# Experts' tails computed row by row, list building divided between one expert and the rest, and a softplus on other engines

## The chip, the cores and the metric

The kernel runs on one core of one Trainium2 chip. The metric is the device time of one execution in microseconds, and the median over several runs is compared. A profile of a single execution goes with it. Five engines matter: TensorE (PE, with PEld for its weight loads), VectorE (DVE), ScalarE (ACT), GpSimd (POOL), and SyncE (SP), which issues most DMAs.

## What is computed

Three stages follow each other (the reference, cut):

```python
for t in range(S):                                   # B=4, H=8, S=768, D=48
    state = alpha[:, :, t, :, None] * state + einsum('bhd,bhe->bhde', k[:, :, t], v[:, :, t])
    y[:, :, t] = einsum('bhd,bhde->bhe', q[:, :, t], state)
x = y as [3072, 384]
noisy = x @ w_gate + log1p(exp(x @ w_noise)) * noise          # 8 experts
top2 of noisy per token; softmax of the two values as weights
for e in range(8):                                            # w1[e] 384x1024, w2[e] 1024x384
    out[rows of e] += weight * (relu(x[rows of e] @ w1[e]) @ w2[e])
return ((out @ w_a) * (out @ w_b)) @ w_out                    # inner width 1536
```

## The kernel before, in words

Products of the expert and the last stage are in fp32 quality: each operand is split into a high and a low part, and `prod3` (L632 to L637) issues three matmuls for one product, on lines L635, L636 and L637. All engines run their instructions in program order, and that order is written out by hand.

**Attention, 24 tiles of 128 tokens.** In step i of the loop, `prep(i+3)` makes two scans on VectorE (D, L460, and A, L464) and two products on GpSimd into the ring of inputs (L462, L465); `sc_unit` (matmuls L490) makes the scores of the next tile, and VectorE masks them into `pm` (L495, two per tile); `intra` (L514) uses `pm`; `u_unit` (L537) and `s_unit` (L549 to L553, the last on GpSimd) carry the state; `gx_unit` and `gm_unit` (L559, L570) make the logits of the gate. Four times in each step `tick()` advances the generators in the list `side` by one piece. `w_tick` loads and splits the first expert's weights into W, one 128x384 piece a step, the split on ScalarE (L112) and GpSimd (L113). It loads at steps 3 to 18 and splits at steps 6 to 21 (`W_FIRST`).

**Routing in two groups, of 14 and 10 tiles.** `route(g)` is such a generator. It computes the softplus as ln(w) with a correction (L229 to L251: two operations on ScalarE, nine on VectorE, all on 128 x 14·8 = 128x112 elements in the first group), the top two (L256 to L264), the ranks by a scan and three matmuls (L270 to L290), and then the lists of tokens for all eight experts: in pieces of at most five tiles, VectorE compares 128 lanes (`at`) and 56 keys (`eqk`, eight experts by seven blocks) with the slots of both choices (L321), multiplies by the token's number (`bt`, L326), and PE sums them (L333). The first group has three such pieces, the second two. Between issue and use lie a few ticks (`LAG`, `RLAG`). `gather` (L368) then fetches 128 rows of x by an indirect DMA that POOL issues.

**Experts.** Expert 0 takes 512 rows from the first 14 tiles, which it can work on while the second group is routed, then 384 rows more. Experts 1 to 7 have 768 rows and a tail of 64 more that is computed only if a flag in `tails` says that the expert has more than 768 tokens. `up_unit` multiplies with w1 (nine matmuls for 128 outputs and 384 or 512 rows), ScalarE (L652) and VectorE (L653) write h into HB; `down_unit` multiplies with w2 (24 matmuls of 384 columns for 128 rows). `up_tail` (L657) holds, under an If on PE (L663), 72 matmuls of 64 columns, with w1 as the stationary operand; its Else is one matmul of 512 columns (L670). `down_tail` (L675) is the last down under a second If. `x_unit` (L376 to L379) transposes the gathered rows of the next expert into X in three PE transposes each.

**Around the experts.** `values_load` reads the eight flags into registers, on all engines for `over` (L853) and on PE for the seven `tails` (L854), all in one place between expert 0's last down and expert 1's first up. Until the experts' end, `bg()` decodes pieces of the last stage's weights, 36 in all, a new one at every third call, on ScalarE (L771, L772, L779), VectorE, GpSimd and two DMAs. Expert 7 goes: up for 512 rows, four downs, the gathers of the last stage's first block, up for 256 rows, `up_tail`, the weighted sums `x2_sum`, the other downs, and with them `split_more` for 36 pieces of the last stage's weights. Then come eight blocks of the last stage (`up2_unit`, `down2_unit`).

Of the kernel before, what the change touches and what calls it, by code (L numbers as in the profile page):

```python
# [36 lines left out]
LAG = 2, 4  # L37
RLAG = 4, 6
HOT = 5
W_FIRST = 3, 6  # L40
# [21 lines left out]
def moe_kernel(ctx: ExitStack, tc, qka0, qka1, afirst, v, wgn, noise, w1, w2, w3, out):  # L62
# [37 lines left out]
    idx = tl(const, [128, E * NJ], I32, "idx")  # L100
    flag = tl(const, [1, 1], I32, "flag")
# [40 lines left out]
    def w_tick(i):  # L142

        if 0 <= i - W_FIRST[0] < 2 * NF1:
            w_load()
        if 0 <= i - W_FIRST[1] < 2 * NF1:
            w_split()
# [23 lines left out]
    idxa = tl(rt, [128, CAPA // 128], I32, "idxa")  # L171
# [44 lines left out]
    def route(g):  # L216
# [10 lines left out]

        gl = tmp("gl", 16)
# [3 lines left out]
        az, ex, w, c, r, ln = (tmp(x) for x in ("az", "ex", "w", "c", "r", "ln"))  # L232
        nc.vector.scalar_tensor_tensor(az, z, -1.0, z, op0=ALU.mult, op1=ALU.max)
        yield
        yield
        nc.scalar.activation(ex, az, AF.Exp, scale=-1.0)
        yield
        yield
        nc.vector.tensor_scalar(w, ex, 1.0, None, op0=ALU.add)
        yield  # L240
        nc.scalar.activation(ln, w, AF.Ln)
# [3 lines left out]
        yield  # L245
        yield
        sp, nl = tmp("sp"), tmp("nl")
        nc.vector.tensor_tensor(sp, ln, c, op=ALU.subtract)
        nc.vector.scalar_tensor_tensor(sp, z, 0.0, sp, op0=ALU.max, op1=ALU.add)
        nc.vector.tensor_tensor(nl, sp, noise_t[:, i0:i0 + n], op=ALU.mult)  # L250
        nc.vector.tensor_tensor(nl, nl, lg, op=ALU.add)  # L251
        yield
        ms, ohs = [], []
        for k in range(2):
# [3 lines left out]
            nc.vector.tensor_tensor(eq, nl, m[:, :, None].to_broadcast(sh), op=ALU.is_equal)  # L258
            nc.vector.tensor_tensor(eq, eq, prio[:, None, :].to_broadcast(sh), op=ALU.mult)
            nc.vector.tensor_reduce(mk, eq, axis=AX.X, op=ALU.max)  # L260
            nc.vector.tensor_tensor(oh, eq, mk[:, :, None].to_broadcast(sh), op=ALU.is_equal)
            if k == 0:
                nl2 = tmp("nl2")
                nc.vector.scalar_tensor_tensor(nl2, oh, -1e30, nl, op0=ALU.mult, op1=ALU.add)  # L264
                nl = nl2
                yield
            ms.append(m)
            ohs.append(oh)
        yield
        nc.vector.tensor_tensor(dm[:, i0:i0 + n], ms[1], ms[0], op=ALU.subtract)  # L270
        oa, xc = tl(rt, [128, E, n + 1], F32, f"oa{n}"), tl(rt, [128, E, n + 1], F32, f"xc{n}", bufs=2)
# [4 lines left out]
        oav = oa[:, :, 1:].rearrange("p e j -> p j e")  # L276
        nc.vector.tensor_tensor(oav, ohs[0], ohs[1], op=ALU.add)
# [3 lines left out]
        for _ in range(RLAG[last]):  # L281
            yield
# [18 lines left out]
        for k in range(2):  # L301
            t = tmp("t")
            nc.vector.tensor_tensor(t, ohs[k], rs, op=ALU.mult)
            nc.vector.tensor_reduce(sf[:, :, k], t, axis=AX.X, op=ALU.add)
        sl = slot[:, i0:i0 + n]
        nc.vector.tensor_copy(sl, sf)
        yield
        pi, ki, pf, kf = tmp("pi", 2, I32), tmp("ki", 2, I32), tmp("pf", 2), tmp("kf", 2)
        nc.vector.tensor_scalar(pi, sl, 127, None, op0=ALU.bitwise_and)
        nc.vector.tensor_scalar(ki, sl, 7, None, op0=ALU.logical_shift_right)  # L310
        nc.vector.tensor_copy(pf, pi)
        nc.vector.tensor_copy(kf, ki)
        yield

        for j0 in range(0, n, HOT):
            m = min(HOT, n - j0)
# [558 lines left out]
    while decs:  # L875
        bg()
# [178 lines left out]
```

## Time and profile before

| what | value |
|---|---|
| three runs | 1122.39, 1128.95, 1122.89 us |
| median | 1122.89 us |
| profiled execution, its own time | 1125.76 us |
| its span | 1124.0 us |
| mean granted TensorE clock | 0.965 of full speed |

The profiled execution takes 1.8 us beyond its span and 2.9 us beyond the median of the runs. The clock is a share of 2.4 GHz: 1.00 is that level, 0.50 would be the level of 1.2 GHz, and a number between says that a stretch had both. PE's columns count a matmul as busy while it is in the pipeline, so that busy matmuls may still be slow ones.

### The profile page before, as it was taken

The page shows a single profiled execution, that of the slowest core. Times are in us where ns is not written, and L with a number is a line of the kernel's source. Part 1 is how long each engine was busy: PE and PEld are TensorE (multiplying, and loading weights), DVE is VectorE, ACT ScalarE, POOL GpSimd, SP SyncE. Part 2 cuts the span into 40 slices and gives each one's busy share as a digit, 9 for nine tenths or more (in the row PEclk, how much of TensorE's full clock was granted, in tenths as well). Part 3 has the DMA queues.
Part 4 walks back from the last instruction along what each step waited for, and adds up shares of the span by engine and source line. Part 5 has one row for each costly group of instructions (what it writes and reads, how often), then busy time and mean ns, then how long its engine had stood idle before and what let it go on. Part 6 is the DMA issues. An engine that isn't in the chain of part 4 may idle for free.

```text
span 1124.0 us, 19331 instructions
## 1 busy us (share of the span) xinstructions
PE 1081.1 (96%) x7610; PEld 1053.0 (94%) x7610; DVE 469.4 (42%) x858; ACT 412.0 (37%) x903; POOL 404.6 (36%) x428
## 2 busy tenths in 40 slices
PE   7987797989999999999999999999999999999998
PEld 5886787989999999999998999999999999999997
DVE  8878938542251445343522246141414141414130
ACT  2444142543352445454534345231313231313231
POOL 5676423563382657574843336010101111100000
PEclk9999698988998999999999899999999999999999
DMA  8999122652452546454533344101010101010000
GB/s 281 231 222 212 37 85 71 186 156 80 127 183 71 168 135 191 138 182 131 189 122 95 106 130 148 36 25 40 22 43 22 43 22 43 16 41 1 22 1 23
DMA packets 62785, 114.58 MB, mean 102 GB/s; under 512 B 8528, under 2 KB 50304, under 8 KB 62688
## 3 DMA queue, kind: packets, MB, share of 16 engines
q1 hardware_dynamic: 56144, 93.49, 28.4%
q0 software_dynamic: 6544, 19.77, 5.7%
q8 instruction: 65, 1.06, 0.4%
q14 instruction: 32, 0.26, 0.1%
HBM read 86.38 MB, written 26.84 MB: 101 GB/s over the span
## 4 chain that ended last, share of the span: by engine, by line
PE 85%; DVE 6%; DMA 4%; issue 3%; ACT 1%; POOL 1%; SPq 0%; POOLq 0%; ACTq 0%; DVEq 0%
PE bank L635 25%; PE bank L636 25%; PE bank L637 25%; PE bank L376 2%; PE bank L490 2%; PE bank L514 2%; DMA wd<-w 1%; DMA wst<-w 1%; PE bank L506 1%; PE bank L482 1%; DMA ring<-qka 1%; DVE D L460 1%; PE bank L537 1%; DVE A L464 1%; DVE at L321 1%
## 5 line engine op out<-in xcount | busy, mean ns | idle before, releaser
L635 PE MATMUL bank<-X,W 128*128 128x384 f32 (+3 forms) x840 | 282.5, 336 | 6.4 <-ACT rf L772 3.0
L636 PE MATMUL bank<-X,W 128*128 128x384 f32 (+3 forms) x840 | 282.3, 336 | 0.1
L637 PE MATMUL bank<-X,W 128*128 128x384 f32 (+3 forms) x840 | 282.2, 336 | 0.0
L113 POOL TENSOR_TENSOR W<-wst,W 128x384 fp32r<-128x384 f32 x136 | 140.0, 1034 | 189.9 <-ACT W L112 179.0
L635 PEld LDWEIGHTS bank<-X,W 128*128 128x128 f32 x840 | 162.3, 193 | 9.9 <-ACT rf L772 3.3
L636 PEld LDWEIGHTS bank<-X,W 128*128 128x128 f32 x840 | 162.4, 193 | 2.5 <-DVE X L379 0.7
L637 PEld LDWEIGHTS bank<-X,W 128*128 128x128 f32 x840 | 162.5, 193 | 1.9
L806 POOL DMA_INDIRECT row<-y,row x48 | 46.2, 962 | 289.9 <-DVE row L814 186.1
L635 PE MATMUL bank<-W,HB 128*128 128x384 f32 x416 | 148.4, 357 | 0.0
L636 PE MATMUL bank<-W,HB 128*128 128x384 f32 x416 | 143.1, 344 | 0.0
L637 PE MATMUL bank<-W,HB 128*128 128x384 f32 x416 | 143.0, 344 | 0.0
L379 DVE TENSOR_TENSOR X<-bank,X 128x384 fp32r<-128x384 f32 (+1 forms) x80 | 42.9, 539 | 204.0 <-ACT X L378 204.0
L917 DVE TENSOR_TENSOR p<-bank,a 128x384 f32<-128x384 f32 x96 | 53.5, 558 | 166.4 <-PE bank L637 166.2
L653 DVE SCALAR_TENSOR_TENSOR HB<-bank,HB 128x384 fp32r<-128x384 f32 (+2 forms) x128 | 71.2, 563 | 90.3 <-ACT HB L652 86.6
L918 ACT ACTIVATE HB<-p 128x384 fp32r<-128x384 f32 x96 | 50.4, 525 | 156.5 <-DVE p L917 156.5
L652 ACT ACTIVATE HB<-bank 128x384 fp32r<-128x384 f32 (+2 forms) x128 | 62.8, 496 | 78.1 <-PE bank L637 77.7
L635 PE MATMUL bank<-EX,HB 128*128 128x384 f32 x240 | 82.0, 342 | 0.0
L635 PEld LDWEIGHTS bank<-W,HB 128*128 128x128 f32 x416 | 80.8, 194 | 0.3
L636 PEld LDWEIGHTS bank<-W,HB 128*128 128x128 f32 x416 | 80.6, 194 | 0.1
L637 PE MATMUL bank<-EX,HB 128*128 128x384 f32 x240 | 80.3, 334 | 0.0
L636 PE MATMUL bank<-EX,HB 128*128 128x384 f32 x240 | 80.3, 334 | 0.0
L637 PEld LDWEIGHTS bank<-W,HB 128*128 128x128 f32 x416 | 80.1, 193 | 0.0
(182 smaller groups left out, 1746.2 us busy)
## 6 DMA issues: line engine op xcount, KB each, us to landing
wst<-w SPq DMA_DIRECT2D x128, 192.0 KB, 3.1
wd<-w SPq DMA_DIRECT2D x36, 384.0 KB, 4.5
ring<-qka SPq DMA_DIRECT2D x36, 288.0 KB, 6.6
y<-o SPq DMA_DIRECT2D x49, 192.0 KB, 1.9
w3f<-u SPq DMA_DIRECT2D x36, 192.0 KB, 2.4
wst<-w3f SPq DMA_DIRECT2D x36, 192.0 KB, 3.0
v<-v SPq DMA_DIRECT2D x24, 192.0 KB, 6.5
xd<-x SPq DMA_DIRECT2D x24, 192.0 KB, 3.8
```

What stands on the lines that cost most here:

```text
L113: eng.tensor_tensor(l, raw, h.bitcast(F32), op=ALU.subtract)
L376: nc.tensor.transpose(pt[:, k * 128:k * 128 + m], t[:m, k * 128:k * 128 + 128], ident[:m, :m])
L379: nc.vector.tensor_tensor(l, ptv, h.bitcast(F32), op=ALU.subtract)
L490: nc.tensor.matmul(pb[h][:, p * 128:p * 128 + 128], part(i, h, NP + p), part(i, h, p), start=True, stop=True)
L635: nc.tensor.matmul(ps, ah, bh, start=first, stop=False)
L636: nc.tensor.matmul(ps, ah, bl, start=False, stop=False)
L637: nc.tensor.matmul(ps, al, bh, start=False, stop=last)
L652: nc.scalar.activation(Hh[:, f, s], pu, AF.Relu)
L653: nc.vector.scalar_tensor_tensor(Hl[:, f, s], pu, 0.0, Hh[:, f, s].bitcast(F32), op0=ALU.max, op1=ALU.subtract)
L806: nc.gpsimd.indirect_dma_start(out=t, out_offset=None, in_=src, in_offset=bass.IndirectOffsetOnAxis(ap=row[:, i, k:k + 1], axis=0))
L917: nc.vector.tensor_tensor(p, ps[1], a, op=ALU.mult)
L918: nc.scalar.activation(Ph[:, f], p, AF.Copy)
```

## The change

1. **Tails.** `up_tail` becomes a generator in two parts. In the first, the last 128 rows of X are the stationary operand and W moves in 512 columns: 18 matmuls into two banks, then relu into `hr`. In the second, after the next down, eight transposes of 64 rows under an If of their own bring `hr` into the form of HB. The Else branches have two 512-column matmuls and one more. For expert 7 the first part stands behind the first half of up, and no longer before the last two downs.
2. **Lists.** `route` builds the lists of expert 0 alone (seven keys, one comparison per token in place of two; for the first group two comparisons with 128 lanes of seven tiles each). A new generator `lists()` builds those for the other experts behind the second group's routing, in five pieces, while expert 0 is computed; its body is the old one. Expert 1's gathers move behind expert 0's second up.
3. **Softplus.** Absolute value, both additions of a constant, the reciprocal (as Exp of -ln) and the relu go to ScalarE; the other six operations, the sum of the two choices and the two products with the ranks go to GpSimd in the first group, and stay on VectorE in the second. `hop` sets the ticks between pieces.
4. **Registers.** One flag is loaded per expert, behind the third of its up units, and `over` in expert 2.
5. **Order of the rest.** W is loaded at steps 3 to 14 and 19 to 22 and split at steps 6 to 17, the last four splits in expert 0's first up; the `bg()` calls of expert 0 go but for its last three downs, and the downs of experts 1 and 2 have two each.

The diff, cut:

```diff
-LAG = 2, 4
-RLAG = 4, 6
+LAG = 3
-W_FIRST = 3, 6
+W_LOAD = [*range(3, 15), *range(19, 23)]
+W_SPLIT = range(6, 18)
...
+        eng = nc.vector if last else nc.gpsimd
...
-        nc.vector.scalar_tensor_tensor(az, z, -1.0, z, op0=ALU.mult, op1=ALU.max)
+        nc.scalar.activation(az, z, AF.Abs)
         nc.scalar.activation(ex, az, AF.Exp, scale=-1.0)
-        nc.vector.tensor_scalar(w, ex, 1.0, None, op0=ALU.add)
+        nc.scalar.activation(w, ex, AF.Copy, bias=1.0)
         nc.scalar.activation(ln, w, AF.Ln)
-        nc.vector.scalar_tensor_tensor(c, w, -1.0, ex, op0=ALU.add, op1=ALU.subtract)
-        nc.vector.reciprocal(r, w)
-        nc.vector.tensor_tensor(c, c, r, op=ALU.mult)
+        nc.scalar.activation(r, ln, AF.Exp, scale=-1.0)
+        nc.scalar.activation(c, w, AF.Copy, bias=-1.0)
+        nc.scalar.activation(mz, z, AF.Relu)
...
+        eng.tensor_tensor(c, c, ex, op=ALU.subtract)
+        eng.tensor_tensor(c, c, r, op=ALU.mult)
+        eng.tensor_tensor(sp, ln, c, op=ALU.subtract)
+        yield
+        eng.tensor_tensor(sp, sp, mz, op=ALU.add)
+        eng.tensor_tensor(nl, sp, noise_t[:, i0:i0 + n], op=ALU.mult)
+        eng.tensor_tensor(nl, nl, lg, op=ALU.add)
...
+        mine = slice(CAPA // 128, NJ) if last else slice(0, CAPA // 128)
+        m = n if n <= 2 * HOT else n // 2
+        for j0 in range(0, n, m):
+            at = tl(rt, [128, HOT, 2, 128], F16, "at").rearrange("p a k w -> p (a k) w")[:, :m]
+            nc.vector.tensor_tensor(at, lane[:, None, :].to_broadcast([128, m, 128]),
+                                    pf[:, j0:j0 + m, None].to_broadcast([128, m, 128]), op=ALU.is_equal)
...
-        if groups[g][-1] == SPLIT - 1:
-            for j in range(CAPA // 128):
-                gather(0, j)
-                yield
         if g == len(groups) - 1:
-            for j in range(CAPA // 128, NJ):
-                gather(0, j)
-            yield
+            yield from lists()
             yield from weights()
...
     def up_tail(e):
-        s = slice(MAIN, CAP)
+        s = slice(CAP - 128, CAP)
         n = CAP - MAIN
-        pu = bank(2 + upn[0] % 4)[:, :NF1 * n]
-        upn[0] += 1
+        w = [W[:, i * 3072:i * 3072 + 3072].rearrange("p (f k n) -> p k f n", f=NF1, k=KD) for i in range(2)]
+        pu = [bank(2 + (upn[0] + i) % 4) for i in range(2)]
+        upn[0] += 2
+        with tc.If(more_rows[e] > 0) as c:
+            for i in range(2):
+                f = slice(4 * i, 4 * i + 4)
+                for k in range(KD):
+                    prod3(pu[i], (Xh[:, k, s], Xl[:, k, s]), (w[0][:, k, f], w[1][:, k, f]), k == 0, k == KD - 1)
+        with c.Else():
+            for i in range(2):
+                nc.tensor.matmul(pu[i], Xh[:, 0, s], w[0][:, 0, 4 * i:4 * i + 4], start=True, stop=True)
...
+        yield
+        pt = trbank()
+        r = slice(128 - n, 128)
         with tc.If(more_rows[e] > 0) as c:
             for f in range(NF1):
-                for k in range(KD):
-                    ks = slice(k * 128, k * 128 + 128)
-                    prod3(pu[:, f * n:f * n + n], (w1h(f)[:, ks], w1l(f)[:, ks]), (Xh[:, k, s], Xl[:, k, s]),
-                          k == 0, k == KD - 1)
+                nc.tensor.transpose(pt[:, f * n:f * n + n], hr[f][r], ident[r, r])
...
@@ expert 0
     for f in range(NF1):
         up_unit(0, f, parts[1])
-        if f < NJ - 4:
-            gather(1, 4 + f)
         if f >= NF1 - 4:
             w_load()
-        bg()
+        tick()
+    while side:
+        tick()
+    for q in range(NJ):
+        gather(1, q)
...
-    over = nc.values_load(flag[0:1, 0:1], min_val=0, max_val=1)
-    more_rows = {e: nc.values_load(tails[0:1, e:e + 1], engines=[mybir.EngineType.PE], min_val=0, max_val=1)
-                 for e in range(1, E)}
+    def load_more_rows(e):
+        more_rows[e] = nc.values_load(tails[0:1, e:e + 1], engines=[mybir.EngineType.PE], min_val=0, max_val=1)
     for e in range(1, E - 1):
         for f in range(NF1):
             up_unit(e, f, [(0, MAIN // 2), (MAIN // 2, MAIN // 2)])
+            if f == 2:
+                load_more_rows(e)
...
-        up_tail(e)
+        tail = up_tail(e)
+        next(tail)
         for j in range(NJ):
             x_unit(e + 1, j)
             if j < NJ - 1:
                 down_unit(e, j)
...
+            next(tail, 0)
```

How the instructions move, at three places. First VectorE in the attention, at the first group's search for the two best experts; `D` and `A` are the scans for a later tile, `pm` the masks for which PE's next scores are used. Before:

```order
L460 SCALAR_TENSOR_TENSOR D_1687<-ring_35_129,bank_30_124 128x512
L463 RECIPROCAL bank_31_125<-D_1687 128x4
L464 SCALAR_TENSOR_TENSOR A_1688<-ring_35_129,bank_31_125 128x512
L256 TENSOR_REDUCE r_m_360_1709<-r_nl_350_1677 128x14
L258 TENSOR_TENSOR r_eq_1711<-r_nl_350_1677,r_m_360_1709 128x112
L259 TENSOR_TENSOR r_eq_1711<-r_eq_1711,prio_105 128x112
L260 TENSOR_REDUCE r_mk_1712<-r_eq_1711 128x14
L261 TENSOR_TENSOR r_oh_363_1713<-r_eq_1711,r_mk_1712 128x112
L495 TENSOR_TENSOR pm_367_1733<-bank_365_1723,causal_72 128x512
L495 TENSOR_TENSOR pm_368_1735<-bank_366_1724,causal_72 128x512
```

The same place in the changed kernel, where the line numbers are its own (L501 for L460, L536 for L495):

```order
L501 SCALAR_TENSOR_TENSOR D_1686<-ring_35_129,bank_30_124 128x512
L504 RECIPROCAL bank_31_125<-D_1686 128x4
L505 SCALAR_TENSOR_TENSOR A_1687<-ring_35_129,bank_31_125 128x512
L264 TENSOR_REDUCE r_m_359_1708<-r_nl_350_1678 128x14
L266 TENSOR_TENSOR r_eq_1710<-r_nl_350_1678,r_m_359_1708 128x112
L536 TENSOR_TENSOR pm_366_1729<-bank_364_1719,causal_72 128x512
L536 TENSOR_TENSOR pm_367_1731<-bank_365_1720,causal_72 128x512
```

Two of the five operations of the search stand ahead of the two masks now, where all five stood there.

Second PE between expert 0's last down and expert 1's first up, where `W_88` with `HB` is a down and `X_95` with `W_88` an up. Before, the rows of one load of `tails` stand seven times:

```order
L637 MATMUL bank_611_3031<-W_88,HB_2326 128x384
L853 TENSOR_LOAD flag_82
L854 TENSOR_LOAD tails_83
L854 ISA x2
L854 TENSOR_LOAD tails_83
L854 ISA x2
```

In the changed kernel a single load stands between two up units of the expert (L676 to L678 are the three lines of `prod3`):

```order
L678 MATMUL bank_619_3128<-X_96,W_89 128x384
L920 TENSOR_LOAD tails_84
L920 ISA x2
L676 MATMUL bank_622_3158<-X_96,W_89 128x384
```

Eight loads in one place became one load in each of eight places.

Third PE at expert 1's tail. Before, the three rows in its middle stand 24 times, and the Else follows:

```order
L663 COMPARE_AND_BRANCH
L635 MATMUL bank_663_3449<-X_95,W_88 128x64
L636 MATMUL bank_663_3449<-X_95,W_88 128x64
L637 MATMUL bank_663_3449<-X_95,W_88 128x64
L663 UNCONDITIONAL_BRANCH
L670 MATMUL bank_663_3449<-X_95,W_88 128x512
L663 UNCONDITIONAL_BRANCH
```

In the changed kernel the three rows stand three times for each of two banks, and after a down the second If follows:

```order
L705 COMPARE_AND_BRANCH
L676 MATMUL bank_651_3336<-W_89,X_96 128x512
L677 MATMUL bank_651_3336<-W_89,X_96 128x512
L678 MATMUL bank_651_3336<-W_89,X_96 128x512
L705 UNCONDITIONAL_BRANCH
L712 MATMUL bank_651_3336<-W_89,X_96 128x512
L712 MATMUL bank_652_3337<-W_89,X_96 128x512
...
L731 COMPARE_AND_BRANCH
L733 MATMUL bank_657_3396<-ident_70,hr_3359 128x64 x8
L731 UNCONDITIONAL_BRANCH
```

72 matmuls of 64 columns became 18 of 512 columns and, one down later, eight transposes.

## Rows read from the trace of the kernel before

**Rows 1.** The page's part 1: busy time, share of the span, instructions.

```profile
PE 1081.1 (96%) x7610; PEld 1053.0 (94%) x7610; DVE 469.4 (42%) x858; ACT 412.0 (37%) x903; POOL 404.6 (36%) x428
```

**Rows 2.** Busy time of each engine by stretch; its columns in the first line.

```profile
core 0: us, PE busy (x) PEld busy (x) DVE busy (x) ACT busy (x) POOL busy (x), PEclk, DMA share, GB/s
75.00:79.70 4.70, 4.70 (x95) 4.41 (x93) 4.63 (x7) 2.49 (x6) 4.49 (x6) 1.00 1.08 241
95.40:146.60 51.20, 40.17 (x560) 36.89 (x558) 43.47 (x83) 15.16 (x35) 26.95 (x28) 0.73 0.43 98
159.20:203.40 44.20, 38.54 (x203) 34.85 (x204) 29.67 (x82) 13.40 (x28) 15.28 (x14) 0.92 0.31 94
234.50:262.30 27.80, 27.80 (x144) 27.80 (x145) 14.18 (x25) 12.63 (x28) 19.11 (x19) 0.89 0.51 158
262.30:279.60 17.30, 17.30 (x101) 17.29 (x100) 2.68 (x6) 2.40 (x5) 2.95 (x3) 0.70 0.07 25
332.10:349.50 17.40, 17.40 (x101) 17.37 (x101) 2.66 (x6) 2.40 (x5) 2.95 (x3) 0.71 0.07 27
377.00:402.00 25.00, 25.00 (x147) 25.00 (x146) 14.59 (x27) 14.94 (x33) 20.78 (x20) 1.00 0.61 190
633.70:650.20 16.50, 16.50 (x105) 16.46 (x104) 2.70 (x5) 3.30 (x8) 4.80 (x5) 0.79 0.22 66
```

**Rows 3.** PE's waits: line, releaser, us in total, times, longest us.

```profile
PE bank L490 <- DVE pm L495: 8.1, 3, 6.3
PE bank L333 <- DVE bt L326: 7.7, 6, 4.6
...
PE bank L635 <- ACT rf L772: 3.0, 1, 3.0
...
PE bank L635 <- DVE HB L653: 1.1, 3, 0.6
```

**Rows 4.** VectorE's groups from 95.4 to 146.6: line, operation, names, count; busy us, mean ns; idle.

```profile
L495 DVE TENSOR_TENSOR pm<-bank,causal 128x512 f32<-128x512 f32 x12 | 7.7, 680 | 0.4 <-PE bank L490 0.4
...
L321 DVE TENSOR_TENSOR at<-lane,r_pf 128x1280 f16<-128x1280 f16 x2 | 2.9, 1474 | 0.0
L321 DVE TENSOR_TENSOR eqk<-keys,r_kf 128x560 f16<-128x560 f16 x2 | 2.5, 1270 | 0.0
...
L326 DVE TENSOR_TENSOR bt<-eqk,token 128x280 f16<-128x280 f16 x4 | 1.6, 447 | 0.1
...
L248 DVE TENSOR_TENSOR r_sp<-r_ln,r_c 128x112 f32<-128x112 f32 x1 | 1.0, 982 | 0.0
...
L250 DVE TENSOR_TENSOR r_nl<-r_sp,noise 128x112 f32<-128x112 f32 x1 | 0.3, 274 | 0.0
```

**Rows 5.** GpSimd's groups from 60 to 152 us.

```profile
L553 POOL TENSOR_TENSOR sc<-ss,aend 128x192 f32<-128x192 f32 x9 | 4.6, 508 | 21.2 <-DVE ss L552 18.1 <-DVE r_pi L309 3.1
```

**Rows 6.** Timeline of GpSimd and VectorE near 109.7 us: start, us, instruction, idle.

```profile
109.69 1.26 POOL L465 TENSOR_TENSOR ring<-ring,A 128x512 f32<-128x512 f32 x1 [0.29 <-DVE A L464]
109.74 1.34 DVE L258 TENSOR_TENSOR r_eq<-r_nl,r_m 128x112 f32<-128x112 f32 x1
```

**Rows 7.** Timeline of PE before expert 1's first up.

```profile
231.14 0.33 PE L637 MATMUL bank<-W,HB 128*128 128x384 f32 x1
234.50 0.68 PE L635 MATMUL bank<-X,W 128*128 128x384 f32 x1 [3.03 <-ACT rf L772]
```

**Rows 8.** PE's groups over the whole span, the third line of a tail's products.

```profile
L637 PE MATMUL bank<-X,W 128*128 128x64 f32 x72 | 23.2, 322 | 0.0
```

**Rows 9.** Timeline of PE at expert 3's Else, which is taken.

```profile
401.98 0.39 PE L670 MATMUL bank<-X,W 128*128 128x512 f32 x1
402.21 0.49 PE L376 MATMUL bank<-ident,row 128*128 128x128 f32 x3
402.46 0.42 PE L635 MATMUL bank<-W,HB 128*128 128x384 f32 x1
```

**Rows 10.** Timeline of PE at the first matmul of the last stage.

```profile
660.63 0.44 PE L635 MATMUL bank<-X,W 128*128 128x384 f32 x1 [1.91 <-ACT X L378]
```

More of the change, by code (lines that the diff above doesn't have):

```diff
@@ L280, in route @@
         carry[0] = xc[:, :, n]
-        for _ in range(RLAG[last]):
+        for _ in range(LAG):
             yield
@@ new lines, in route @@
+        nc.vector.tensor_tensor(bt, eq, val[:, :, None].to_broadcast([128, n, NJ]), op=ALU.mult)
+        yield
+        mine = slice(CAPA // 128, NJ) if last else slice(0, CAPA // 128)
[4 more added lines that the diff above has]
+                                    pf[:, j0:j0 + m, None].to_broadcast([128, m, 128]), op=ALU.is_equal)
+            for _ in range(LAG):
+                yield
+            pl = spot(1, NJ)
+            for j in range(m):
+                nc.tensor.matmul(pl, at[:, j], bt[:, j0 + j], start=j == 0, stop=j == m - 1)
+            acc = lacc[:, mine]
+            nc.vector.tensor_tensor(idx0[:, mine] if j0 + m == n else acc, pl[:, mine], acc, op=ALU.add)
@@ new lines, in route, with lists @@
+        yield
+        for j in range(*mine.indices(NJ)):
+            gather(0, j)
+        yield
+        for k in range(2):
+            t = tmp("t")
+            eng.tensor_tensor(t, ohs[k], rs, op=ALU.mult)
+            for _ in hop(2):
+                yield
+            nc.vector.tensor_reduce(sf[:, :, k], t, axis=AX.X, op=ALU.add)
+        nc.vector.tensor_copy(slot[:, i0:i0 + n], sf)
+        yield
+    def lists():
+        pi, ki, pf, kf = (tl(rt, [128, NT, 2], dt, x) for x, dt in (("ei", I32), ("ri", I32), ("rf", F32), ("e1", F32)))
+        nc.vector.tensor_scalar(pi, slot, 127, None, op0=ALU.bitwise_and)
+        nc.vector.tensor_scalar(ki, slot, 7, None, op0=ALU.logical_shift_right)
+        nc.vector.tensor_copy(pf, pi)
+        nc.vector.tensor_copy(kf, ki)
+        for j0 in range(0, NT, HOT):
+            m = min(HOT, NT - j0)
@@ new lines, in up_tail @@
+        with c.Else():
+            for i in range(2):
+                nc.tensor.matmul(pu[i], Xh[:, 0, s], w[0][:, 0, 4 * i:4 * i + 4], start=True, stop=True)
+        hr = []
+        if e < E - 1:
+            t = tl(dec, [128, 2, 512], F32, "hr")
+            for i in range(2):
+                nc.scalar.activation(t[:, i], pu[i], AF.Relu)
+                hr += [t[:, i, q * 128:q * 128 + 128] for q in range(4)]
+        else:
+            for q, m in ((0, 3), (3, 3), (6, 2)):
+                t = tl(rows, [128, DM], F32, "row")
+                for i in range(2):
+                    a, b = max(q, 4 * i), min(q + m, 4 * i + 4)
+                    if a < b:
+                        nc.scalar.activation(t[:, (a - q) * 128:(b - q) * 128],
+                                             pu[i][:, (a - 4 * i) * 128:(b - 4 * i) * 128], AF.Relu)
+                hr += [t[:, c * 128:c * 128 + 128] for c in range(m)]
@@ L828, in moe_kernel @@
         mid = {}
-        if j == NA - 2:
-            while side:
-                tick()
-            for q in range(4):
-                gather(1, q)
         if j == NA - 1:
@@ L858, in moe_kernel @@
             up_unit(e, f, [(0, MAIN // 2), (MAIN // 2, MAIN // 2)])
+            if f == 2:
+                load_more_rows(e)
+            if e == 2 and f == 5:
+                over = nc.values_load(flag[0:1, 0:1], min_val=0, max_val=1)
             if f < NJ:
@@ L886, in moe_kernel @@
             load_more()
+    tail = up_tail(e)
+    next(tail)
     for j in range(NA):
         down_unit(e, j)
+        next(tail, 0)
     for j in range(TB):
```

107 lines of the change are left out of this document (56 added, 51 removed).

## The prediction

> **What bounds the kernel now.** I read the page's busy times first. PE is busy for 1081.1 us of the span (96%), twice as long as any other engine [rows 1], so the time can fall only where PE idles, runs below its full clock, or does work that can be made smaller. The windows show where that is [rows 2]. A free attention step (75.00 to 79.70) takes 4.70 us, with VectorE busy for 4.63 and GpSimd for 4.49 of it: attention is bound by those two. From 95.40 to 146.60, where the first group is routed, six steps (12 masks, two per step [rows 4]) take 51.20 us instead of 6 x 4.70 = 28.2; VectorE is busy for 43.47, PE's clock has dropped to 0.73. PE's waits [rows 3] name the cause: 8.1 us for `pm`, the longest 6.3, and 7.7 us for `bt`. Later, 159.20 to 203.40, PE idles for 44.20 - 38.54 = 5.7 us at a clock of 0.92. Before expert 1's up PE stands still for 3.03 us [rows 7]. Its first up then takes 27.80 us where expert 3's takes 25.00. Last come the two stretches of 17.30 and 17.40 us with a tail each, at 0.70: 72 matmuls of 64 columns on each of `prod3`'s three lines over the kernel [rows 8], which is 24 for each of three tails that are taken (experts 1, 2 and 7); the other four take their Else.
>
> The changed kernel's time is the profiled execution's own, 1125.8, plus the terms below. That execution is 2.9 us above the median of the runs, which I take off at the end.
>
> **Term A: attention with the first group's routing.** VectorE loses nine softplus operations on 112 elements, 0.27 to 0.98 us each [rows 4], 3.9 together; the sum of the choices and two products, three more at 0.27 to 0.33, 0.9; and the three list pieces. A full piece costs 1.47 (`at`) + 1.27 (`eqk`) + 2 x 0.45 (`bt`) + 0.2 for the sum = 3.8, the three together 11.2. With 1.2 for the operations on both choices' slots that is 17.2. It gains two `at` of 7 x 128 = 896 elements, 0.7 x 1.47 = 1.03 each, and small ones of 14 to 98 elements, 4.0 in all. So 13.2 us leave the engine that has no free time in these steps. The order also puts the masks ahead of three of the five search operations, which shortens the waits for `pm`. I take -14. What speaks against more is GpSimd: nine operations of 112 elements move to it, and it is busy for 4.49 of 4.70 us where a step is free. The nearest row, 192 elements in 0.508 us [rows 5], gives about 0.3 each, 2.7 in all; spread over three steps and with W's split already moved elsewhere, half is hidden. Were all of it and a wait on GpSimd's queue exposed, A would be -6; with every wait gone as well, and the clock at 1.00, -19.
>
> **Term B: expert 0 and expert 1's up.** The second group's routing and the lists stay on VectorE here, where it is busy for 29.67 of 44.20 us. What can go: 5.7 us of idle time, 0.08 x 44.20 = 3.5 of clock, 3.0 at the registers, and 27.80 - 25.00 = 2.8 in expert 1's up, together 15.0. What comes in: five pieces for 24 tiles, where two were built, are 28 more matmuls of 56 columns; by the 101 of 17.30 us they can't take more than 0.17 each, 4.8, and at the full clock I take 2.2. The last pieces meet the second up, where VectorE also has its evictions: three ticks per up unit of 9 x 25.00/144 = 1.6 us, five per piece, make a piece every 2.6 us, and VectorE needs 3.8 for one, which I count as 3 us of waiting at PE. B = -15.0 + 5.2 = -9.8. If expert 0's idle time stays it is -5, if the lists are wholly hidden -14. For the registers: eight loads in a row cost the 3.03 us that show and a part that the matmuls queued ahead of them hid. If that part is as long, an estimate, the eight take 6 us and one takes 0.75, and a single load with 3 us of matmuls ahead of it is hidden.
>
> **Term C: the tails of experts 1 and 2.** A matmul of 512 columns follows the last after 402.21 - 401.98 = 0.23 us [rows 9], so 18 take 4.1. Three transposes take 402.46 - 402.21 = 0.25, a down of 24 matmuls 24 x 25.00/144 = 4.2, and eight transposes, by the three, at most 0.9. That is 9.5 where 17.30 and 17.40 stood, so -7.8 and -7.9, or -15.7. It rests on the clock: the low level in these stretches came with 64-column matmuls, 512-column ones hold 1.00 elsewhere. At the clock of now they would take 9.5/0.70 = 13.6 and a tail would save 3.7; without any transposes on the path it would save 8.7. The wait for `hr` is covered by the down between the two parts: 4.2 us against two relus of 512 elements, and ScalarE is idle for most of that stretch.
>
> **Term D: the tails not taken.** Each of experts 3 to 6 has two more matmuls of 512 columns, 0.46, and one more If; four make +1.8 (0 to +3, if the extra branch costs a few tenths).
>
> **Term E: expert 7.** Its tail and one down take 16.50 at a clock of 0.79. With the tail moved behind the first up they become 4.1 + 0.9 + 0.2 + 4.2 = 9.4, so -7.1. But PE's next work is the last stage, which waits for 1.91 us now, on ScalarE's copy of X [rows 10], behind the 36 splits of weights. Those get 7.1 us less before it, and I count 1.8 back: -5.3. If the whole chain is on the path, only -1 is left; if none of it, -6.5.
>
> **Term F: the decodes.** Two `bg()` per down put twice the work of ScalarE, VectorE and GpSimd in the downs of experts 1 and 2, and some decodes end at expert 6's end. Three waits for HB cost 1.1 together now, so about 0.4 each [rows 3]; I add four of them, +1.5 (0 to +3). The other parts (gathers for expert 1 behind its second up, all seven at once, ahead of W's splits on GpSimd) I cost at nothing, since expert 0's last three downs, 12.6 us, hide them; if they don't, PE waits for X at expert 1's first up, up to 4.
>
> Sum: -14 - 9.8 - 15.7 + 1.8 - 5.3 + 1.5 = -41.5. 1125.8 - 41.5 = 1084.3; less 2.9 this is 1081.4, or 1081.
>
> **The rivals.** *R1, GpSimd stops VectorE.* At 109.69 us a product on GpSimd runs for 1.26 us, and VectorE's comparison that started 0.05 later takes 1.34 [rows 6], against 0.27 for a like operation [rows 4]; it ends with the other. So operations that meet last as long as both, and nine more of them sit on GpSimd, where also the state's product waits in the queue. If each of the nine makes VectorE lose its own 0.5 us and a step's chain then waits on GpSimd for as much again, 9 more us go, and with 3 for masks that come late as before A is -2, the time 1081 + 12 = 1093. For it: that meeting. Against it: 13 us leave VectorE, so there are fewer to meet. Chance 0.12.
>
> The Trainium skill (SBUF — State Buffer, section SBUF: two separate sides) says that VectorE and GpSimd share a pair of ports as an exclusive lock, held for a whole instruction and also against a VectorE operation with two inputs in SBUF. By that rule both products and additions here block such operations, and the time would be the one of R1; the meeting at 109.69 agrees with it (1.34 instead of 0.27).
>
> *R2, the waits of expert 0 stay.* Expert 0's second up now holds the lists' end, the gathers for expert 1 follow, and PE waits there instead of before: 5.7 stay, the clock falls as now (3.5), and the gathers come late by 1: +10, 1091. For it: VectorE is late in that stretch already, and five pieces are more than two. Against it: expert 0's first up, four downs and half its second up lie before the lists' use. Chance 0.10.
>
> *R3, the slower side: each register load stops PE.* If the stop before expert 1's up is the cost of stopping at all and not of eight loads, then eight places pay it. At the 6 us of the whole stop, 8 x 6 = 48 us come in, and the gain of 3 counted in B goes: 1081 + 48 + 3 = 1132. It decides from (1123 - 1084)/8 = 4.9 us a stop. For it: rows show a stop only with eight loads together. Against it: the wait ends with what eight loads in series take, and the sequencer's lead covers one. Chance 0.03.
>
> *R4, more is won.* With the attention's steps free of waits (A = -18) and the lists hidden (B = -14): 1081 - 8 = 1073. For it: 51.20 - 28.2 = 23 us are lost there now. Against it: GpSimd's 4.49 of 4.70. Chance 0.13.
>
> **How the numbers follow.** The forecast has 0.62, R1 0.12, R2 0.10, R4 0.13, R3 0.03. Its own bounds come from A (-19 to -6), B (-14 to -5), C (-17 to -7), E (-6.5 to -1), which don't all fall to one side: 1074 to 1089. The range takes in R2 and R1 with some of their spread and R4: 1069 to 1097. A measurement tells about 1% (11 us) from no change. All cases but R3 lie more than 1% below 1122.9 with room, so faster 0.95; a mixture of R1 and R2 with little from the tails would be within 1%, 0.03; slower is R3 with 0.02, the rest of its chance being stops of 3 to 5 us, which are within 1%.
>
> **What would show it.** Right: waits of L536's masks and of the list matmuls under 3 us in all, PEclk near 1.0 in the attention's last third; no 64-column group, 18 matmuls of 512 columns at 0.23 us per tail; no 3 us stop ahead of expert 1; six steps with the first group's routing in under 40 us. Wrong: C falls if the tails' matmuls run at the low clock or their second If waits for `hr`; A falls if GpSimd's small operations last over 1 us or VectorE's masks still wait; B falls if PE waits at the list matmuls in expert 0's second up; the whole is wrong if a gap of some us stands at each load of a flag.

## The result, and the profile after

The changed kernel takes 1095.8 us (median of four runs, 1093.1 to 1100.3); its runs relate to those of the kernel before as 0.9743 (95% interval 0.9694 to 0.9793). The forecast was 1081 with a range of 1069 to 1097: faster, and inside the range, but at its upper end and outside the forecast's own 1074 to 1089. The profiled execution took 1097.9 us with a span of 1096.2, 27.8 less than before; 41.5 had been summed. So 13.7 us are missing, and the first question is where. The median lies 1.2 us inside the range while the four runs spread over 7.2, so that it came out inside is in part luck. One of the ten runs with the old tails below (1130.5 us, at a lower granted clock) is left out of its numbers.

PE's waits in the changed kernel, in the form of [rows 3] (L531 is before's L490, L536 its L495, L382 its L333, L676 its L635, L694 its L653):

```profile
PE bank L676 <- DVE HB L694: 6.6, 6, 3.4
PE bank L531 <- DVE pm L536: 5.0, 3, 3.2
...
PE bank L676 <- ACT X L425: 2.9, 1, 2.9
...
PE bank L300 <- DVE xc L291: 2.5, 1, 2.5
PE bank L382 <- DVE bt L375: 1.7, 3, 0.9
...
PE bank L676 <- ACT HB L693: 1.4, 1, 1.4
```

The waits for `pm` and `bt` fell from 8.1 and 7.7 us to 5.0 and 1.7. New are 6.6 for HB (1.1 before), 2.5 for `xc`, the scan that the second group's ranks are made from, and 1.4 ahead of expert 0's first down. The same by stretch, in the form of [rows 2]: attention from the 16th tile on, expert 0's first up, four downs, second up and three downs, expert 1's up and tail, expert 3's up, expert 7's first up, the first up of the last stage.

```profile
core 0: us, PE busy (x) PEld busy (x) DVE busy (x) ACT busy (x) POOL busy (x), PEclk, DMA share, GB/s
95.20:142.58 47.38, 41.73 (x696) 38.53 (x694) 35.91 (x70) 17.53 (x41) 30.40 (x38) 0.89 0.50 125
...
146.47:169.85 23.38, 19.54 (x89) 15.65 (x89) 15.41 (x44) 8.04 (x19) 4.09 (x4) 0.93 0.00 0
169.85:188.52 18.67, 18.67 (x125) 18.29 (x126) 11.39 (x25) 2.95 (x6) 3.14 (x3) 1.00 0.20 65
188.52:204.88 16.36, 14.43 (x101) 13.23 (x101) 11.67 (x31) 4.04 (x9) 4.42 (x5) 1.00 0.34 99
204.88:220.09 15.21, 15.21 (x95) 14.69 (x94) 5.30 (x10) 7.78 (x18) 8.19 (x9) 1.00 0.56 173
220.10:245.05 24.95, 24.95 (x145) 24.95 (x145) 13.37 (x25) 14.44 (x32) 21.37 (x21) 1.00 0.64 201
245.05:249.40 4.35, 4.35 (x22) 3.55 (x22) 2.17 (x3) 2.04 (x5) 2.09 (x3) 1.00 0.14 52
345.00:372.00 27.00, 24.98 (x144) 24.66 (x143) 14.12 (x27) 15.24 (x34) 22.48 (x22) 1.00 0.57 180
563.70:583.80 20.10, 16.68 (x73) 13.49 (x73) 9.53 (x13) 10.82 (x24) 14.23 (x14) 1.00 0.53 160
631.10:645.70 14.60, 14.45 (x73) 14.19 (x74) 4.73 (x8) 4.67 (x10) 2.91 (x4) 0.88 0.25 74
```

Expert 1's up is at 24.95 us, as expert 3's was before, and the tail's 18 matmuls and the three transposes behind them take 4.35 at the full clock (2.4 GHz). Expert 7's first up, 72 matmuls of 512 columns or 72 x 0.23 = 16.6 us, takes 20.10. Expert 3's up takes 27.3 us from its first matmul to the next stage's (the window shown leaves out its edges), against 25.0 before.

The whole difference of the two profiled executions, from the start of PE's first matmul of one stage to that of the next:

| stage | before | after | difference | the term and its forecast |
|---|---|---|---|---|
| to expert 0's first up | 159.17 | 146.47 | -12.7 | A -14 |
| expert 0 | 75.33 | 73.62 | -1.7 | B -7.0 (its part without expert 1's up) |
| expert 1's up | 27.82 | 24.96 | -2.9 | B -2.8 |
| tails and downs of experts 1 and 2 | 89.74 | 74.13 | -15.6 | C -15.7 |
| Elses and downs of experts 3 to 6 | 113.08 | 115.17 | +2.1 | D +1.8 |
| expert 7 behind its first up | 52.45 | 47.28 | -5.2 | E -5.3 |
| ups of experts 2 to 6, expert 7's first | 143.04 | 149.46 | +6.4 | F +1.5 |
| last stage | 463.4 | 465.1 | +1.7 | none |

The differences sum to the span's -27.8, within rounding. A, C, D and E came close to their forecasts; how much of that is luck is said further below. Of the missing 13.7 us, 5.3 lie in expert 0, 4.9 in the ups, 1.7 in the last stage, where a low clock (0.88) follows the wait for X, and 1.3 in A. The experiments ask first whether the terms that agree do so for the reasons given, and then what holds expert 0 and the ups.

### The profile page after: what moved, and what is told of

It is laid out like the page before. It is cut to its first block, busy times and chain, and to the rows that moved or that the text cites. A ratio compares the mean times of both kernels' runs of the same rounds, so it can differ in the third digit from the quotient of the medians.

```text
span 1096.2 us, 19170 instructions
## 1 busy us (share of the span) xinstructions
PE 1055.5 (96%) x7504; PEld 1022.0 (93%) x7504; DVE 481.5 (44%) x860; ACT 422.1 (39%) x929; POOL 407.6 (37%) x437
## 4 chain that ended last, share of the span: by engine, by line
PE 84%; DVE 6%; issue 3%; DMA 3%; ACT 2%; POOL 2%; SPq 0%; POOLq 0%; DVEq 0%; ACTq 0%
PE bank L676 24%; PE bank L677 24%; PE bank L678 24%; PE bank L531 2%; PE bank L423 2%; PE bank L555 2%; PE bank L547 1%; PE bank L523 1%; DMA wst<-w3f 1%; DMA wd<-w 1%; PE bank L578 1%; DVE HB L694 1%; DVE pm L536 1%; DMA wst<-w 1%; DVE u L840 1%
## 5 line engine op out<-in xcount | busy, mean ns | idle before, releaser
L676 PE MATMUL bank<-X,W 128*128 128x384 f32 (+2 forms) x768 | 260.6, 339 | 10.0 <-DVE HB L694 6.6
L677 PE MATMUL bank<-X,W 128*128 128x384 f32 (+2 forms) x768 | 259.5, 338 | 0.3 <-DVE X L426 0.2
L678 PE MATMUL bank<-X,W 128*128 128x384 f32 (+2 forms) x768 | 259.4, 338 | 0.0
L676 PEld LDWEIGHTS bank<-X,W 128*128 128x128 f32 x768 | 145.2, 189 | 14.2 <-DVE HB L694 8.6
L677 PEld LDWEIGHTS bank<-X,W 128*128 128x128 f32 x768 | 145.2, 189 | 2.7 <-DVE X L426 0.8
L678 PEld LDWEIGHTS bank<-X,W 128*128 128x128 f32 x768 | 145.1, 189 | 2.1
L676 PE MATMUL bank<-W,HB 128*128 128x384 f32 x416 | 145.4, 350 | 1.4 <-ACT HB L693 1.4
L677 PE MATMUL bank<-W,HB 128*128 128x384 f32 x416 | 140.8, 338 | 0.0
L678 PE MATMUL bank<-W,HB 128*128 128x384 f32 x416 | 140.8, 338 | 0.0
L694 DVE SCALAR_TENSOR_TENSOR HB<-bank,HB 128x384 fp32r<-128x384 f32 (+2 forms) x128 | 70.1, 562 | 69.3 <-ACT HB L693 68.8
L676 PE MATMUL bank<-EX,HB 128*128 128x384 f32 x240 | 82.1, 342 | 0.0
L678 PE MATMUL bank<-EX,HB 128*128 128x384 f32 x240 | 80.3, 335 | 0.0
L676 PEld LDWEIGHTS bank<-W,HB 128*128 128x128 f32 x416 | 78.1, 188 | 1.8 <-issue 1.4
L415 POOL DMA_INDIRECT row<-xd,idx x56 | 60.6, 1082 | 51.4 <-DVE ei L390 25.6
L997 DVE TENSOR_TENSOR HB<-p,HB 128x384 fp32r<-128x384 f32 x96 | 53.6, 559 | 56.8 <-ACT HB L996 56.8
```

The source lines that it names most:

```text
L415: nc.gpsimd.indirect_dma_start(out=t[:m], out_offset=None, in_=xd[:SPLIT * 128] if a else xd, in_offset=bass.IndirectOffsetOnAxis(ap=ix, a ...
L676: nc.tensor.matmul(ps, ah, bh, start=first, stop=False)
L677: nc.tensor.matmul(ps, ah, bl, start=False, stop=False)
L678: nc.tensor.matmul(ps, al, bh, start=False, stop=last)
L694: nc.vector.scalar_tensor_tensor(Hl[:, f, s], pu, 0.0, Hh[:, f, s].bitcast(F32), op0=ALU.max, op1=ALU.subtract)
L997: nc.vector.tensor_tensor(Pl[:, f], p, Ph[:, f].bitcast(F32), op=ALU.subtract)
```

## Experiments

**The tails as before.** Edit: the old `up_tail` at its old places in the changed kernel.

```diff
...
-                nc.tensor.transpose(pt[:, f * n:f * n + n], hr[f][r], ident[r, r])
+                for k in range(KD):
+                    ks = slice(k * 128, k * 128 + 128)
+                    prod3(pu[:, f * n:f * n + n], (w1h(f)[:, ks], w1l(f)[:, ks]), (Xh[:, k, s], Xl[:, k, s]),
+                          k == 0, k == KD - 1)
...
-        tail = up_tail(e)
-        next(tail)
+        up_tail(e)
...
```

> The changed kernel with the tails computed as before (72 matmuls of 64 columns a line, W stationary, expert 7's tail behind its second up). Theory: the tails' gain is local, by columns and clock. From expert 1's tail to expert 2's first up PE needs 37.1 us in the changed kernel and 44.8 again here, the same for expert 2 (37.1 to 44.9), at a granted clock near 0.7 in the stretch with the tail; expert 7 loses 5; experts 3 to 6 win 0.5 each: +18.6 in all, some 1114. Rival: the quicker tails were in part given back as waits for HB in the next up (0.5 us in expert 2, 2.0 in expert 3), and those go here: +16. Rival: the low clock came from something else than the 64-column matmuls; then the clock is near 1.0 here and each tail costs only 3 more: +8.

Measured: 1115.8 us (nine runs), 0.9953 of the kernel before (0.9916 to 0.9990), so the tails are some 20 us of the changed kernel's gain. The first tail with its downs takes 46.5 us, the second 44.9, against 37.1 each in the changed kernel, and expert 7's part is 5.2 longer. The windows of the two tails, with the next expert's first transposes, and the down behind each:

```profile
240.10:252.70 12.60, 12.60 (x77) 12.60 (x76) 2.15 (x3) 2.10 (x5) 2.07 (x3) 0.64 0.05 18
252.70:258.50 5.80, 5.80 (x23) 5.80 (x22) 1.99 (x4) 0.77 (x2) 0.00 (x0) 0.61 0.00 0
313.60:324.60 11.00, 11.00 (x76) 11.00 (x75) 2.53 (x4) 1.18 (x3) 2.21 (x3) 0.73 0.19 45
324.60:330.30 5.70, 5.70 (x23) 5.70 (x22) 1.17 (x2) 0.81 (x2) 0.00 (x0) 0.62 0.00 0
```

The clock falls to 0.61 to 0.73 in and behind the old tails, though PE is busy without a gap, and stays at 1.00 in the new ones and the downs behind them. The low clock does come with these matmuls. The waits for HB in experts 2 and 3 remain with the old tails (1.7 and 2.2 us), so the quicker tails don't make them, and the first rival falls.

**The softplus on VectorE.** Edit: `eng = nc.vector` for both groups, the order of the program untouched.

```diff
-        eng = nc.vector if last else nc.gpsimd
+        eng = nc.vector
```

> The changed kernel with the first group's nine GpSimd operations on VectorE. Theory: VectorE bounds these steps, so its relief counts: the six steps with the first group's routing take 43.0 us in the changed kernel and some 46 here (nine operations of 0.27 to 1.0 us), the whole +3. Rival (the two engines stop each other): the operations on GpSimd cost VectorE as much as they relieve it, the six steps stay within 1 us of 43.0 or fall.

Measured: 1096.1 us (1093.0 to 1099.1), no difference from the changed kernel's 1095.8. From the 16th tile's intra to the 22nd's it takes 38.2 us. The changed kernel takes 37.9, and the run with later ranks (below), whose attention is the changed kernel's, 37.8. (The 43.0 of the expectation are seven steps, to the 23rd tile's intra; this run takes 43.2 for them.) First this run, then the one with later ranks:

```profile
89.40:127.60 38.20, 33.04 (x546) 30.28 (x544) 33.79 (x69) 13.42 (x31) 22.23 (x24) 0.91 0.49 122
90.30:128.10 37.80, 32.84 (x544) 30.52 (x542) 32.46 (x62) 13.42 (x31) 24.91 (x31) 0.86 0.49 130
```

VectorE has seven more operations here and is busy for 1.3 us more, 0.2 each, not the 3 that were expected. So small a difference is below what the attention varies by from run to run (see the end). GpSimd needs 0.42 us for each, where 0.3 was estimated. That GpSimd's operations delay VectorE as much as they relieve it is not shown by this: both theories allow a difference so small.

**The lists of all experts in the routing.** Edit: the old list code with all 56 keys and both choices behind the ranks of each group, and no `lists()`; softplus, tails and the rest as changed.

```diff
...
         yield from route(g)
+        if groups[g][-1] == SPLIT - 1:
+            for j in range(CAPA // 128):
+                gather(0, j)
+                yield
         if g == len(groups) - 1:
-            yield from lists()
+            for j in range(CAPA // 128, NJ):
+                gather(0, j)
+            yield
             yield from weights()
```

> The changed kernel with the lists of all eight experts built per group in the routing, as before; softplus, tails and the rest as changed. Theory: three pieces of 3.8 us return to VectorE in the attention in place of two comparisons: from the 16th tile's intra to the first up of expert 0 +8 to +10; expert 0 loses its three further pieces: -3 in its second up (16.4 us to 13); total +6. Rival: the lists only moved from one place to the other and the total stays within 2 us.

Measured: 1101.4 us (1099.6 to 1104.0), 5.6 above the changed kernel's median. From the 16th tile's intra to expert 0's first up it takes 60.9 us, 51.3 in the changed kernel and no more than 57.2 in any other profile with the lists apart. That stretch varies by 8 us, so the steps in which the pieces stand say more: from the 20th tile's intra to the 23rd's this run takes 28.0 us, and the nine other profiles of versions with the lists apart take 16.8 to 18.4. First this run, then the changed kernel:

```profile
117.52:145.50 27.98, 21.50 (x303) 20.10 (x301) 17.80 (x38) 6.80 (x15) 11.56 (x14) 0.70 0.19 58
121.36:138.19 16.83, 15.07 (x289) 13.93 (x287) 10.95 (x27) 6.57 (x15) 8.24 (x8) 1.00 0.28 86
```

VectorE is busy for 6.9 us more there, and PE's clock is 0.70 instead of 1.00. Expert 0's second up takes 12.7 us instead of 16.4. So the lists make most of the attention's gain, some 10 us, and what was moved of them costs 3.6 us in expert 0. Both numbers are near the expected ones.

**The flags at once.** Edit: all eight loads ahead of expert 1's first up.

```diff
+    over = nc.values_load(flag[0:1, 0:1], min_val=0, max_val=1)
+    for e in range(1, E):
+        load_more_rows(e)
...
-            if f == 2:
-                load_more_rows(e)
...
```

> The changed kernel with all eight flags loaded in one place ahead of expert 1's first up. Theory: eight loads in a row outlast the matmuls queued ahead: PE stands still for 3 us there again, total +3. Rival: the stop of before was the wait for a decode's weights (its releaser was rf, L772): there is no stop, total 0.

Measured: 1106.6 us (1099.2 to 1113.2), 10.8 more than the changed kernel where 3 were expected, with a spread too wide for 3 us. The timeline of PE at the place is plain:

```profile
223.49 0.33 PE L678 MATMUL bank<-W,HB 128*128 128x384 f32 x1
227.62 0.44 PE L676 MATMUL bank<-X,W 128*128 128x384 f32 x1 [3.80 <-issue]
```

The stop of 3.03 [rows 7] is back as 3.80 us and no longer put down to a decode; expert 1's up behind it takes 26.7 instead of 24.95. That is 5.5 of the 12.3 us by which the two profiled executions differ. Most of the rest stands where the edit changes nothing: 3.7 ahead of expert 0's first up and 2.5 in expert 7's, which vary so in other runs too. In the changed kernel no gap stands at any of the eight single loads.

**What holds expert 0's first up.** VectorE and GpSimd in the changed kernel at the start of the second group's softplus:

```profile
149.94 1.01 POOL L114 TENSOR_TENSOR W<-wst,W 128x384 fp32r<-128x384 f32 x1 [8.73 <-ACT W L113]
150.09 0.96 DVE L252 TENSOR_TENSOR r_c<-r_c,r_ex 128x80 f32<-128x80 f32 x1
151.09 0.24 DVE L253 TENSOR_TENSOR r_c<-r_c,r_r 128x80 f32<-128x80 f32 x1
```

The first of two like operations takes 0.96 us and ends with GpSimd's split of W, the second 0.24. Four operations of this chain are stretched so, once for each of the four splits that the change put here, 2.8 us in all. The second candidate is the lag between the scan and the ranks: in the second group it was six ticks before (`RLAG = 4, 6`) and is three now (`LAG = 3`). Two runs ask whether the collisions or the shorter lag make PE wait for `xc`. The first takes the splits out, the second gives the six ticks back:

```diff
-W_SPLIT = range(6, 18)
+W_SPLIT = [*range(6, 18), *range(20, 24)]
```

> The changed kernel with the last four splits of expert 0's weights in the attention's last four steps in place of expert 0's first up. Theory 1: in the first up GpSimd's splits stretch four of VectorE's routing operations from 0.24 to 0.94 us, so the search ends late and PE waits 2.45 us for xc: here they last 0.24, the wait is under 0.7, and from expert 0's first up to its first down 23.4 us become 20; the attention's last steps grow by 0 to 1.5; total -2. Theory 2 (three ticks are too few between scan and ranks in the second group): the wait stays at 2 or more, total 0 to +1.

```diff
-        for _ in range(LAG):
+        for _ in range(LAG + 3 * last):
```

> The changed kernel with six ticks instead of three between the second group's scan and its rank matmuls. Theory 2 (too few ticks): the wait of 2.45 us for xc goes and nothing takes its place: total -2. Theory 1 (the routing's chain on VectorE is late by itself): the wait goes, but the lists come three ticks later and PE waits as long for them in expert 0's downs or second up: total 0.

Measured: with the splits elsewhere every operation of the chain takes 0.23 to 0.24 us, the wait for `xc` is gone and expert 0's first up with its waits takes 19.0 us instead of 23.4; in all 1093.9 us (1092.0 to 1094.2). With the later ranks the wait is gone too, and the up takes 17.3. First the run with the splits moved, then the one with later ranks:

```profile
143.70:162.70 19.00, 17.62 (x89) 14.51 (x89) 12.63 (x44) 6.35 (x15) 0.00 (x0) 1.00 0.00 0
143.10:160.40 17.30, 17.30 (x79) 14.28 (x79) 12.24 (x34) 7.44 (x18) 4.09 (x4) 1.00 0.00 0
```

In the run with the later ranks also the wait ahead of the first down is gone: PE does no list matmul at the end of the up, and the bank that the down needs is free. Expert 0 takes 68.7 us (69.3 with the splits moved) instead of 73.6; in the other profiles that leave its code alone it takes 71.9 to 75.1. The waits for the lists are 1.1 us, so neither the lists nor the gathers come too late. So both causes are needed: the chain was late by the collisions, and three ticks left no room for that; removing either is enough for the wait. The times of these two runs don't show the gain of 4.9 clearly (1093.9 and 1096.2 against 1095.8). With the later ranks, expert 7's first up took 22.8 instead of 20.1 us (at a clock of 0.85) and expert 3's 29.0 instead of 27.3, where nothing was changed. In both runs the way from the 22nd tile's intra to expert 0's first up took 1.6 more than in the changed kernel, so the moved splits can't be blamed for it.

**What holds the ups.** VectorE's, GpSimd's and PE's timeline in the changed kernel ahead of expert 7's wait of 3.42 us, which ends at 575.52:

```profile
572.50 0.99 POOL L848 TENSOR_TENSOR rf<-rf,ah 128x384 f32<-128x384 f32 x1
...
573.53 1.33 DVE L850 SCALAR_TENSOR_TENSOR u<-wd,rf 128x384 int32<-128x384 int32 x1 [2.26 <-POOL rf L848]
...
574.79 1.27 DVE L694 SCALAR_TENSOR_TENSOR HB<-bank,HB 128x512 fp32r<-128x512 f32 x2
...
575.52 0.50 PE L676 MATMUL bank<-X,W 128*128 128x512 f32 x1 [3.42 <-DVE HB L694]
```

A decode's last step (L850) waits for its steps on GpSimd, and the evictions (L694), for which PE waits, stand behind it on VectorE. The change dropped 20 `bg()` calls in expert 0 and added 14. 107 are left, and 36 decodes need 110 (a new one at every third call, five calls each), so the loop that empties the decodes at expert 6's end issues three steps in a row. First edit: the double calls in expert 3 too.

```diff
-            if e < 3:
+            if e < 4:
                 bg()
```

> The changed kernel with two decode calls per down in expert 3 as well, so that no decode is left at expert 6's end. Theory: the 3.4 us wait for HB in expert 7's first up comes from the leftover decode steps, issued one behind the other and ahead of the evictions on VectorE: the wait goes, expert 7's first up falls from 20.1 to 16.4 us, total -3. Rival: the wait moves to expert 4's up (as 2.0 us stand in expert 3's now): total -1. Rival: the wait in expert 7 comes from W's splits on GpSimd and stays.

Measured: 1095.8 us (1092.6 to 1099.1). Expert 7's first up takes 16.4 us, its wait is gone; but expert 4's up takes 32.5 instead of 25.5, with this wait:

```profile
405.54 0.69 PE L676 MATMUL bank<-X,W 128*128 128x384 f32 x1 [4.09 <-DVE HB L694]
```

The first rival was right on where the wait goes, and its size was under-estimated; the second, W's splits, is out for expert 7, since the wait there is gone with the splits in place. In each case the stalled up follows a last down with a double call (expert 3 behind 2, expert 4 behind 3), where also W's splits are doubled. Expert 2 stands behind such a down as well and waits for 0.5 us only, so this is a guess at the place and not yet a cause. Hence the next edit, which puts no double call there and yet makes 111:

```diff
-            if e < 3:
+            if e < 4 and j < NJ - 1:
                 bg()
```

> The changed kernel with the second decode call in the first six of each seven downs of experts 1, 2 and 3, and none in the last. Theory: the waits for HB arise where decode steps issued one behind the other stand on VectorE ahead of an up's evictions, be it leftovers ahead of expert 7 (3.4 us) or a double call in an expert's last down (2.0 in expert 3; 4.1 moved to expert 4 when only expert 3 got double calls as well). With both gone no wait for HB is over 0.7 us, expert 3's and 4's ups take under 26, expert 7's first up 16.5: -5.5 against the changed kernel over the stretch from expert 1's first up to the last stage, the whole -5. Rival: as many decodes as these can't be placed in three experts, and a wait of 2 or more stands in another up; total -1 to -3.

Measured: 1094.9 us (1090.4 to 1096.9). Expert 3's and expert 7's waits are gone (25.0 and 16.4 us). In expert 4's up waits of 1.8 and 0.7 us stand, though no double call is ahead of it, and it takes 28.0 us where under 26 was expected and 25.5 stood in the changed kernel: the rival is right in part. From expert 1's first up to the last stage it takes 406.2 us instead of 411.0: -4.8 of the -5.5. The profiled execution's whole shows nothing of it, since in it the attention's end from the 16th tile on took 57.2 us instead of 51.3.

**Both.** The edits of the last run and of the later ranks together.

> The changed kernel with both: the decodes spread as in the run before and six ticks instead of three ahead of the second group's ranks. Theory: the gains lie in different places and add: from expert 0's first up to expert 1's 69 us (73.6 in the changed kernel), and -5.5 later, the whole some -9, a median near 1086. Rival: a later second group makes expert 1's gathers late or shifts the ticks so that a wait returns; total -5.

Measured: 1086.4 us (six runs, 1083.8 to 1088.4), 0.9611 of the kernel before (0.9574 to 0.9648); that interval lies wholly below the changed kernel's. Expert 0 takes 68.8 us, expert 1's first up to the last stage 405.6 (411.0), so 4.8 and 5.4 come out as in the single runs, and this version beats both kernels. PE's waits behind the attention:

```profile
PE bank L676 <- ACT X L425: 2.3, 1, 2.3
PE bank L676 <- DVE HB L694: 2.2, 2, 1.8
PE bank L382 <- DVE bt L375: 1.4, 4, 0.7
...
```

## Why the prediction was right, and where it was off

The forecast's signs came out mixed. There are 18 matmuls of 512 columns at 0.23 us per tail, no stop stands ahead of expert 1, and the six steps that took 51.2 us take 37.9, under the 40 that were named. But the waits for the masks and the lists are 5.0 + 1.7 = 6.7 us and not under 3, and the clock in the attention's last third is 0.89 and not near 1.0. One reading of the rows was wrong without touching the sum: of the 7.7 us for `bt`, 5.3 (0.69 at 186.00 and 4.60 at 191.35) stood in expert 0's downs and not in the attention.

- *Term A, -14: measured -12.7.* The mechanism is shown for the lists: with them back, three steps of the attention take 28.0 us instead of 16.8 to 18.4. That the number is so close is luck: in the seven profiles whose code is the same up to there, expert 0's first up starts between 140.0 and 150.1 us, which would make A anything from -9 to -19. One step of its sum was over-sized, "nine softplus operations on 112 elements, 0.27 to 0.98 us each [rows 4], 3.9 together": the 0.98 was an operation lengthened by a meeting with GpSimd, and VectorE is relieved of 1.3 us for seven of the moved operations. What the softplus on ScalarE and the order of the masks gave was not taken apart and drowns in the spread.
- *Term B, -9.8: measured -1.7 - 2.9 = -4.6, short of its own bound of -5* (which by its terms, -9.8 + 5.7 of idle time that stays, should read -4.1). This step failed. The idle time of the downs went as counted (27.8 us became 18.7), the registers' 3 us and the 2.8 of expert 1's up too, and the second up grew by 3.7 us where 5.2 were allowed. But I counted new waits only at the lists, "which I count as 3 us of waiting at PE", and those are 1.7. I put expert 0's first up at nothing, though the change laid the last four splits of W beside the second group's search there and cut the ticks between its scan and its ranks from six to three. It cost 2.5 us of waiting for `xc`, 1.4 ahead of the first down, the ranks' and list matmuls that now stand there, and a clock of 0.93: expert 0's first up took 23.4 us instead of 16.5. With the six ticks back expert 0 takes 68.7 us, 6.6 less than before, where 7.0 were forecast.
- *Term C, -15.7: measured -15.6.* Both parts are shown: fewer columns, and the clock, 0.61 to 0.73 in and behind the old tails and 1.00 in the new ones.
- *Term D, +1.8: measured +2.1,* four times 0.52; the further If costs next to nothing.
- *Term E, -5.3: measured -5.2,* and the run with the old tails shows the same 5.2. Two misses cancel in it: the tail and the downs gained 6.2 us instead of 7.1, and the wait before the last stage grew by 1.0 (1.9 to 2.9) instead of 1.8. The low clock behind that wait, which added 1.5 us in the last stage, was in no term.
- *Term F, +1.5: measured +6.4, outside its 0 to +3.* This step failed too. The step "I add four of them", waits of 0.4 each, took the size from rows in which decode steps come one at a time. Pairs of calls and a loop that empties the rest let several of them stand ahead of an eviction, and the longest waits are 2.0 and 3.4 us. I had seen that some decodes end at expert 6's end and hadn't counted how many calls were left: 107 for 110.
- *The rivals.* R3 (each load stops PE) is out: the loads apart cost nothing, the loads together 3.8 us. R4 did not come. R2 had the right place with another cause: 1.7 us of waits at the lists, 2.5 at the search, and gathers in time. R1's meetings exist, but where they decided, with the shorter lag, was expert 0's first up; in the attention the moved operations changed the time by less than its spread.

## What to carry to other kernels

Count for every moved piece of background work what is queued behind it on its engine: a decode step that waits for another engine holds the evictions behind it. Here that cost 0.6 us at most while such steps came one at a time, and 2.0 to 4.1 us where several came together. When a change frees an engine in one stage, look at the next stage for work that now arrives earlier there, or beside something else that the change has put in the same place. When a change shortens the lag of a chain that PE waits for, check that nothing else has made that chain longer; the three ticks that were taken away here cost 4.9 us together with four collisions. And look for narrow matmuls at a low clock: the same products with the wide operand moving cost 4 us here instead of 10 to 12.

## What the runs showed of the hardware

Within the same code the attention's end differs from run to run by 8 us, and the granted clock goes with it. From the 16th tile's intra to expert 0's first up, in two runs whose code is the same up to there (51.3 us in the changed kernel):

```profile
91.42:148.57 57.15, 51.72 (x761) 47.26 (x759) 35.66 (x73) 20.66 (x48) 27.11 (x36) 0.80 0.44 110
```

```profile
90.24:140.00 49.76, 43.20 (x761) 38.87 (x759) 37.77 (x74) 20.30 (x48) 30.09 (x38) 0.97 0.53 143
```

The first, from the run with the decodes spread, has a clock of 0.80, the second, with the double calls in expert 3, one of 0.97, with the same 761 matmuls. VectorE is busy for less in the slower one, so it isn't the bound there. Five more profiles with this attention lie between 48.9 and 55.5 us. What sets the clock's course in these steps stays open; changes of some 3 us were therefore read from their own stage and not from the whole time.

The Trainium skill (SBUF — State Buffer, section SBUF: two separate sides) says that VectorE and GpSimd share a pair of ports as an exclusive lock held for a whole instruction, also against a VectorE operation with two inputs in SBUF. The trace agrees at 150.09: 0.96 us beside GpSimd's split of 1.01, 0.24 without one.
